# Batch 0's token-major scores computed by TensorE, first loads in longer rows, opening reordered: an attention and feed-forward kernel on one core

## The chip, the core and the metric

The kernel runs on one core of one Trainium2 chip. The metric is the device time of one execution in microseconds, the median of several runs. The core's engines are named as in the profile: PE (TensorE; PEld are its weight loads), DVE (VectorE), ACT (ScalarE), POOL (GpSimd) and SP (SyncE, here only an issuer of DMAs).

## What is computed

```python
B, H, S, Ns, D = (8, 8, 512, 32, 64)            # x: B,H,S,D   state: B,H,Ns,D
def _attn_ref(x, state):
    scores = scale * x @ state.T                 # tokens look at 32 state rows
    a = softmax(scores); xread = a @ state
    scores2 = scale * state @ x.T                # state rows look at 512 tokens
    a2 = softmax(scores2); sread = a2 @ x
    return concatenate([xread, sread], axis=2)   # B,H,544,D

def _moe_ref(x, w_in, w_out):                    # x: 4352 rows of 512
    h = x @ w_in                                 # 512 x 2048, float64 in memory
    g = h - tanh(h)
    return g @ w_out                             # 2048 x 512, float64 in memory
```

The attention output, with its heads joined, is the input of the feed-forward layer. Inputs x and state are float32, the two weight matrices are float64 and are turned to float32 on the chip.

## The kernel before

The feed-forward layer works through nine chunks of rows: eight batches of 512 tokens (chunks 0 to 7) and, last, the 256 rows that the state rows give. Each chunk has 16 hidden tiles (a 128-row piece of the 2048 hidden features): `hidden` makes h of one tile on PE, ACT makes tanh, DVE subtracts, and `output` multiplies with a row block of w_out. Products with state are folded into w_in: m = state times w_in, so that the attention weights multiply m directly. The whole program is built once; a scheduler sets the order on each engine, except where `tc.keep_in_program_order` or `tc.issue_after` pins it.

The change is in the opening, before the first hidden tile of chunk 0. Its order is written out by hand: `SEQ` is a string of two-letter steps, a letter for the operation and a number for its piece, and `step` issues each. What is shown as `tps`, `sps`, `mps` and so on in the rows are PSUM tiles of these steps:

- D: a matmul on zeros (`warm`), which only keeps PE busy.
- S0, S1: scores of batch 0 with state rows in partitions (`sps`), for heads 0 to 3 and 4 to 7: two matmuls of 128x64 weights (a block-diagonal `bdr` of state) and 512 columns each. c0, c1: ACT copies them to SBUF (`s`).
- T0, T1: the same scores with tokens in partitions (`tps`). In the kernel before these are four 128x128 transposes of the copy `s` (line 735).
- M, B, E, Z, z, q, N: softmax over the 32 state rows: DVE maximum (line 738), DVE subtraction (`e`, line 742), ACT exponential, DVE sum, add, reciprocal, DVE scaling (line 753).
- A, y: four PE transposes back (`aps`, line 758) and ACT's copy to `at`.
- a, b, r, p: the four instructions that turn one float64 weight block to float32: two integer operations on DVE (lines 136 and 137), one on ACT (line 138, tiles named w00r, wo0r and so on), one custom sum on DVE (line 139). Numbers 0 to 3 are the first 512 columns of w_in (blocks w00 to w03), 4 and 5 the first two row blocks of w_out (wo0, wo1). A `p` of 0 to 3 also writes the converted block to DRAM (`wf`), for use much later, and every `p` issues the next weight load.
- m, k, R: m of the first 512 hidden features on PE (`mps`, lines 792 and 783) and ACT's copies of it to SBUF.
- h0 to h3, H0 to H3: hidden tiles 0 to 3 of chunk 0 (`hps`, line 808), first and second half of the heads. X is their tanh, x their subtraction (`g`, line 815). After them PE goes on with `output` of chunk 0 (`ops`, line 604 and following).

All loads of the opening are on SP's DMA queue, but for one of 256 KB on ACT's. A weight block lands in one of six raw buffers (`parts`, four, and `twins`, two), so a load waits on SP until the block that was in its buffer is converted, and everything behind it on SP waits with it. The converted blocks are written to two rotating tiles (tag `wf`, two buffers of two blocks each): whoever writes such a tile again waits until its DRAM writes have been read out.

Of the kernel before, what the change touches and what calls it, by code (L numbers as in the profile page):

```python
# [9 lines left out]
F32 = mybir.dt.float32  # L10
# [27 lines left out]
@with_exitstack  # L38
def attention_ffn(ctx: ExitStack, tc: tile.TileContext, xT, xn, x0, bh, sp, sm, win, wout, xout, tout, sout):

# [47 lines left out]
    def bank(p, name):  # L88
        return p.tile([P, 512], F32, tag=p.name, name=name)
# [7 lines left out]
    def big(name, shape, dtype):  # L97
        return pool.tile(shape, dtype, tag="big", name=name, bufs=BIG)
# [7 lines left out]
    class Weight:  # L106
# [4 lines left out]

        def load(self):
            if self.src.dtype == F32:
                self.raw = next(raws)(f"{self.name}d", [P, 512], F32)
                dst = self.raw
            else:
                self.raw = next(raws)(f"{self.name}d", [P, 512, 2], U32)
                dst = self.raw.rearrange("p f w -> p (f w)")
            src = self.src.bitcast(dst.dtype)
            if len(src.shape) == 3:  # L120
                dst = dst.rearrange("p (r f) -> p r f", r=4)
            loadlog.append(nc.sync.dma_start(dst, src).ins)

# [518 lines left out]
    def advance(units, n=1):  # L642
# [7 lines left out]
    w0 = [  # L650
        [Weight(win[r * P : r * P + P, 512 * q : 512 * q + 512], f"w{q}{r}") for r in range(DM // P)]
        for q in range(NQ)
    ]

    w0[0] = [
        Weight(win[:, j * P : j * P + P].rearrange("(r p) f -> p r f", p=P), f"w0{j}") for j in range(4)
    ]
    wos = [Weight(wout[f * P : f * P + P], f"wo{f}") for f in range(NFF)]
    wfs = {}

    def convert_win(q, p):
        if p % 2 == 0:
            wfs[q, p // 2] = pool.tile([P, 2, 512], F32, tag="wf", name=f"w0{q}{p // 2}", bufs=WB)
        made = w0[q][p].convert(wfs[q, p // 2][:, p % 2])
        if p % 2:
            nc.sync.dma_start(wf[q][:, p - 1 : p + 1], wfs[q, p // 2])
        return made
# [18 lines left out]
    def o(x):  # L686
        tc.keep_in_program_order(x)
        if x.ins.engine == mybir.EngineType.DVE:
            firstDVE[0] = x.ins

    aTs[0] = pool.tile([P, 2, 2, 512], F32R, tag="aT0", name="aT0", bufs=1)
    sps = pool.tile([P, 4, P], F32, tag="sm", name="sps", bufs=1)
    xb = big("x00", [P, 768], F32)
    xrs = [pool.tile([P, 2, 512], F32, tag="x", name=f"xT0{hf}", bufs=XB) for hf in range(2)]
    nc.sync.dma_start(xb, x0)
    nc.scalar.dma_start(xrs[0][:, 1], xT[0, 0][:, 1])
    load(1)
    nc.sync.dma_start(xrs[1], xT[0, 1])
    nc.sync.dma_start(sps, sp[0])
    load(4)  # L700
    bdr = xb[:, :256].rearrange("p (i m) -> p i m", i=4)
    moving = {(0, 0): xb[:, 256:]} | {(j, c): xrs[j][:, c] for j, c in ((0, 1), (1, 0), (1, 1))}

# [13 lines left out]
    def step(op):  # L717
# [3 lines left out]
        elif k == "S":  # L721
            sps_ps[j] = bank(ps_o, f"sps0{j}")
            for c in range(2):
# [6 lines left out]
        elif k == "T":  # L730

            tps[j] = bank(ps_o, f"tps0{j}")
            for t in range(4):
                cols = slice(P * t, P * t + P)
                o(nc.tensor.transpose(tps[j][:, cols], ss[j][:, cols], ident))
        elif k == "M":
# [25 lines left out]
        elif k in "abrp":  # L762
            if j not in csteps:
                if j > 3:
                    if j == 4:
                        plain[0] = big("wp0", [P, 2, DM], F32)
                    csteps[j] = wos[j - 4].steps(plain[0][:, j - 4])
                else:
                    if j % 2 == 0:
                        wb[j // 2] = pool.tile([P, 2, 512], F32, tag="wf", name=f"w00{j}", bufs=WB)  # L770
                    csteps[j] = w0[0][j].steps(wb[j // 2][:, j % 2])
# [3 lines left out]
            if k == "p" and j < 4:  # L775
                w = wb[j // 2][:, j % 2].rearrange("p (r f) -> p r f", r=4)
                nc.sync.dma_start(wf[0][:, :, j * P : j * P + P], w)
        elif k == "m":
# [41 lines left out]
    MP = [{"a": ps_a, "o": ps_o}[x] for x in 'oaoa']  # L820
    SEQ = 'D D D D D b0 S0 D a0 c0 T0 S1 D M0 r0 B0 p0 m0 E0 c1 r1 Z0 T1 R0 b1 a1 z0 p1 q0 a2 k0 b2 r2 N0 m1 p2 A0 r3 M1 k1 R1 y0 r4 b3 B1 a3 m2 E1 p3 Z1 r5 h1 h0 m3 k2 z1 q1 h2 N1 A1 a5 k3 y1 h3 R2 b4 H0 R3 b5 H1 X0 H2 X1 a4 H3 p5 p4 x0 x1'
    for op in SEQ.split():
# [521 lines left out]
```

## Time and profile before

| | |
|---|---|
| median of 3 runs | 629.43 us (629.32 to 630.81) |
| the profiled execution: its own time | 629.0 us |
| its span (first to last instruction) | 627.2 us |
| PE busy | 621.5 us, 99% of the span, 3610 matmul records |
| DVE busy | 488.8 us, 78% |
| ACT busy | 370.4 us, 59% |
| POOL busy | 38.7 us, 6% |

A float32 matmul leaves two records in the trace (two passes), a transpose and a matmul on float32r operands one. PE's records have a modelled end; the distance between starts tells how fast it works. A row of the timeline can merge several records of one kind, with their number behind the x; its duration is from the first start to the last end. Idle time before a row stands in brackets with what ended it.

### The profile page before, as it was taken

Reading aid. Unit: us, or ns where it says so; the run is one execution under the profiler, and the core shown is the slowest. Engines: PE = TensorE matmul, PEld = TensorE weight load, DVE = VectorE, ACT = ScalarE, POOL = GpSimd, SP = SyncE. Lnnn points to the kernel's source line nnn. Section 1 sums busy time; section 2 is a strip of 40 time slices with the busy share of each in tenths; the row PEclk is TensorE's granted clock in tenths of the full one; section 3 lists DMA queues with packets and bytes.
Section 4 is the critical chain, followed back from the end, with each engine's and each line's share of the span. In section 5 each row is a group of like instructions: output and inputs, shape, how many; then the busy total and the mean of one; then the engine's idle time right before and its main releaser. Section 6 shows DMA issues by size and latency. Waiting matters only on the chain.

```text
span 627.2 us, 9849 instructions
## 1 busy us (share of the span) xinstructions
PE 621.5 (99%) x3610; PEld 490.9 (78%) x3610; DVE 488.8 (78%) x781; ACT 370.4 (59%) x613; POOL 38.7 (6%) x66
## 2 busy tenths in 40 slices
PE   8999999999999999999999999999999999999997
PEld 5456677788888788778886678788888888888997
DVE  5999998799697696998357679988955878764582
ACT  5876777678666475755346785447555543562642
POOL 0000002132311000000000000000000000010000
PEclk9999999999999999999999999999999999999999
DMA  9993875869988857999716996765555675699990
GB/s 318 354 390 135 302 245 145 256 194 341 291 278 287 280 177 262 319 315 397 253 34 217 338 345 212 228 209 168 176 168 183 201 187 164 201 260 341 410 337 26
DMA packets 68672, 155.90 MB, mean 249 GB/s; under 512 B 6032, under 2 KB 27920, under 8 KB 68624
## 3 DMA queue, kind: packets, MB, share of 16 engines
q1 hardware_dynamic: 62400, 134.04, 63.7%
q0 software_dynamic: 6080, 20.98, 11.5%
q8 instruction: 28, 0.46, 0.3%
q10 hardware_dynamic: 144, 0.26, 0.1%
q14 instruction: 20, 0.16, 0.1%
HBM read 110.69 MB, written 44.56 MB: 248 GB/s over the span
## 4 chain that ended last, share of the span: by engine, by line
PE 96%; DVE 2%; ACT 1%; issue 0%; ACTq 0%
PE X L1067 14%; PE hps L553 10%; PE hps L554 10%; PE hps L555 10%; PE ops L606 8%; PE ops L608 8%; PE ops L607 8%; PE Y0m L1067 5%; PE Y1m L1067 5%; PE mps L263 2%; PE mps L179 2%; PE X L1173 2%; PE ops L604 2%; PE Y8m L1173 1%; PE rps L501 1%; PE hps L808 1%
## 5 line engine op out<-in xcount | busy, mean ns | idle before, releaser
L606 PE MATMUL ops<-wo,g 128*128 128x512 f32 x244 | 95.5, 396 | 0.0
L607 PE MATMUL ops<-wo,g 128*128 128x512 f32 x244 | 95.2, 390 | 0.0
L553 PE MATMUL hps<-aT,m 128*128 128x512 f32 x240 | 94.7, 397 | 0.0
L554 PE MATMUL hps<-aT,m 128*128 128x512 f32 x240 | 93.8, 391 | 0.1
L555 PE MATMUL hps<-aT,m 128*128 128x512 f32 x240 | 93.8, 391 | 0.0
L608 PE MATMUL ops<-wo,g 128*128 128x512 f32 x244 | 88.3, 393 | 0.0
L568 ACT ACTIVATE t<-hps 128x512 f32<-128x512 f32 x64 | 38.4, 601 | 57.9 <-PE hps L555 57.2
L568 DVE TENSOR_TENSOR G<-hps,t 128x512 f32<-128x512 f32 x64 | 43.8, 687 | 36.8 <-ACT t L568 36.7
L606 PEld LDWEIGHTS ops<-wo,g 128*128 128x128 f32 x244 | 45.7, 188 | 15.6 <-issue 1.9
L553 PEld LDWEIGHTS hps<-aT,m 128*128 128x128 f32 x240 | 45.0, 188 | 14.5 <-issue 2.5
L580 DVE TENSOR_TENSOR t<-hps,t 128x512 f32<-128x512 f32 x61 | 41.7, 683 | 18.4 <-ACT t L580 18.0
L104 ACT CAST g<-t 128x512 fp32r<-128x512 f32 x61 | 37.8, 619 | 28.5 <-DVE t L580 27.9
L608 PEld LDWEIGHTS ops<-wo,g 128*128 128x128 f32 x244 | 45.6, 188 | 10.8 <-DVE wo L104 0.8
L555 PEld LDWEIGHTS hps<-aT,m 128*128 128x128 f32 x240 | 45.0, 188 | 11.0 <-issue 1.7
L607 PEld LDWEIGHTS ops<-wo,g 128*128 128x128 f32 x244 | 45.8, 188 | 9.9 <-DVE wo L104 0.3
L554 PEld LDWEIGHTS hps<-aT,m 128*128 128x128 f32 x240 | 45.1, 188 | 9.7 <-DVE aT L104 0.5
L580 ACT ACTIVATE t<-hps 128x512 f32<-128x512 f32 x61 | 36.4, 597 | 26.3 <-PE hps L555 25.9
L1067 PE MATMUL X<-g0m,W0m 128*128 128x512 f32 x192 | 47.9, 390 | 0.0
L104 DVE TENSOR_TENSOR g<-t,g 128x512 fp32r<-128x512 f32 x61 | 41.6, 684 | 7.1 <-ACT g L104 6.9
L1067 PE MATMUL X<-g1m,W1m 128*128 128x512 f32 x192 | 45.8, 389 | 0.0
L104 ACT CAST g1m<-G 128x1024 fp32r<-128x1024 f32 x28 | 29.2, 1056 | 27.6 <-PE Y1m L1067 10.9
L1067 PEld LDWEIGHTS X<-g0m,W0m 128*128 128x128 f32 x192 | 36.0, 188 | 8.3 <-issue 0.8
(279 smaller groups left out, 1155.4 us busy)
## 6 DMA issues: line engine op xcount, KB each, us to landing
w<-wf POOLq DMA_DIRECT2D x32, 256.0 KB, 6.5
mm<-st POOLq DMA_DIRECT2D x16, 512.0 KB, 6.3
xn<-in_xn SPq DMA_DIRECT2D x16, 512.0 KB, 5.8
mr<-mm SPq DMA_DIRECT2D x16, 512.0 KB, 5.1
wsd<-ws SPq DMA_DIRECT2D x16, 512.0 KB, 7.7
wod<-wo SPq DMA_DIRECT2D x32, 256.0 KB, 6.6
W0m<-wsd SPq DMA_DIRECT2D x16, 512.0 KB, 3.7
W1m<-wsd SPq DMA_DIRECT2D x16, 512.0 KB, 3.9
```

What stands on the lines that cost most here:

```text
L104: return nc.scalar.copy(hi, src), (sub or nc.vector).tensor_sub(lo, src, hi)
L179: made = nc.tensor.matmul(pss[b][rows], sp2[r, p + c, 64 * b + at : 64 * b + at + 32], w[r, c], start=True, stop=True,)
L553: nc.tensor.matmul(ps, mhi[k][:, cols], ahi[:, k], start=(k == 0), stop=False)
L554: nc.tensor.matmul(ps, mhi[k][:, cols], alo[:, k], start=False, stop=False)
L555: made = nc.tensor.matmul(ps, mlo[k][:, cols], ahi[:, k], start=False, stop=(k == nk - 1))
L568: main(nc.scalar.activation(t, ps, AF.Tanh), nc.vector.tensor_sub(g, ps, t))
L580: tanhs.append((nc.scalar.activation(t, ps, AF.Tanh).ins, nc.vector.tensor_sub(t, ps, t).ins))
L606: nc.tensor.matmul(o, g[:, 0, tok], w[:, 0], start=(f in self.begins), stop=False)
L607: nc.tensor.matmul(o, g[:, 0, tok], w[:, 1], start=False, stop=False)
L608: return nc.tensor.matmul(o, g[:, 1, tok], w[:, 0], start=False, stop=stop).ins
L1067: made = nc.tensor.matmul(out[t], w[:, e, x, cols], y[:, e], start=first and j == 0 and e == 0 and c == 0, stop=last and j == 3 and e == 1 ...
L1173: made = nc.tensor.matmul(out, o[:, x, s], w[:, y], start=first and jp == 0 and s == 0 and c == 0, stop=last and jp == 1 and s == 3 and c ...
```

## The change

Batch 0's x arrives in one load of 640 KB with the block-diagonal state ahead of it (128 rows of 5 KB), in place of 384 KB on SP's queue and 256 KB on ACT's. Weight block w00 goes to ACT's queue instead. The first 512 columns of w_in come as an input of their own, laid out so that each of w00 to w03 is 128 rows of 4 KB in place of 512 rows of 1 KB. T0 and T1 are eight matmuls each of x (the stationary operand, 128 tokens) with the block-diagonal state (64 columns), straight from the loaded x; the copies c0 and c1 remain for the state rows' own softmax, which comes later. The DRAM writes of w00 to w03 go from SP's queue to POOL's (`pooled`). Block w10 (the next columns of w_in) gets its four steps in the opening as number 6. The string SEQ has a new order with two steps D fewer.

```diff
-        def load(self):
+        def load(self, queue=nc.sync):
...
-            loadlog.append(nc.sync.dma_start(dst, src).ins)
+            loadlog.append(queue.dma_start(dst, src).ins)
...
-    w0[0] = [
-        Weight(win[:, j * P : j * P + P].rearrange("(r p) f -> p r f", p=P), f"w0{j}") for j in range(4)
-    ]
+    w0[:0] = [[
+        Weight(w0b[j], f"w0{j}") for j in range(4)
+    ]]
...
-    xb = big("x00", [P, 768], F32)
-    xrs = [pool.tile([P, 2, 512], F32, tag="x", name=f"xT0{hf}", bufs=XB) for hf in range(2)]
+    xb = pool.tile([P, 1280], F32, tag="aT1", name="x00", bufs=1)
+    xr = pool.tile([P, 2, 512], F32, tag="x", name="xT01", bufs=XB)
     nc.sync.dma_start(xb, x0)
-    nc.scalar.dma_start(xrs[0][:, 1], xT[0, 0][:, 1])
-    load(1)
-    nc.sync.dma_start(xrs[1], xT[0, 1])
+    next(loads).load(nc.scalar)
+    nc.sync.dma_start(xr, xT[0, 1])
...
-            sps_ps[j] = bank(ps_o, f"sps0{j}")
+            sps_ps[j] = bank(ps_h, f"sps0{j}")
...
             for t in range(4):
-                cols = slice(P * t, P * t + P)
-                o(nc.tensor.transpose(tps[j][:, cols], ss[j][:, cols], ident))
+                for c in range(2):
+                    cols = slice(P * t + 64 * c, P * t + 64 * c + 64)
+                    o(nc.tensor.matmul(
+                        tps[j][:, cols], moving[j, c][:, P * t : P * t + P], bdr[:, 2 * j + c], start=True, stop=True
+                    ))
...
-                if j > 3:
-                    if j == 4:
+                if j == 6:
+                    wfs[1, 0] = pool.tile([P, 2, 512], F32, tag="wf", name="w010", bufs=WB)
+                    csteps[j] = w0[1][0].steps(wfs[1, 0][:, 0])
+                elif j > 3:
+                    if 0 not in plain:
...
-                nc.sync.dma_start(wf[0][:, :, j * P : j * P + P], w)
+                pooled(wf[0][:, :, j * P : j * P + P], w)
...
-    SEQ = 'D D D D D b0 S0 D a0 c0 T0 S1 D M0 r0 B0 p0 m0 E0 c1 r1 Z0 T1 R0 b1 a1 z0 p1 q0 a2 k0 b2 r2 N0 m1 p2 A0 r3 M1 k1 R1 y0 r4 b3 B1 a3 m2 E1 p3 Z1 r5 h1 h0 m3 k2 z1 q1 h2 N1 A1 a5 k3 y1 h3 R2 b4 H0 R3 b5 H1 X0 H2 X1 a4 H3 p5 p4 x0 x1'
+    SEQ = 'D D D D D r0 T0 b0 a0 M0 S0 B0 p0 T1 m0 E0 r1 Z0 a1 r2 b1 z0 p1 b2 q0 R0 a2 r3 S1 m1 c0 k0 N0 p2 A0 y0 M1 a3 B1 b3 m2 k1 c1 h1 h0 p3 R1 E1 k2 Z1 z1 r6 q1 r4 m3 N1 h2 k3 A1 h3 y1 H0 b5 a5 r5 R3 X0 H1 R2 H2 a6 a4 b4 p4 b6 X1 x0 H3 p5 x1'
...
-            turn = convert_win(1, p)
+            turn = convert_win(1, p, csteps.get(6) if p == 0 else None)
...
-    x0 = c(np.concatenate([bd[0].reshape(P, 256), xT[0, 0, :, 0]], axis=1))
+    x0 = c(np.concatenate([bd[0].reshape(P, 256), xT[0, 0].reshape(P, 2 * S)], axis=1))
...
+    w0b = c(win[:, :512].reshape(4, P, 4, P).transpose(2, 1, 0, 3).reshape(4, P, 512))
+    win = c(win[:, 512:])
```

On PE, from the first matmul to the first hidden tile, these stand in a row before (tps 135 and 168 are T0 and T1, sps S0 and S1, mps 153, 190 and 223 m0 to m2, aps 203 is A0, hps 1 is h1):

```order
L720 MATMUL warm<-const-float32-0.0 128x256 x5
L724 MATMUL sps_128<-x_101 64x512
L724 MATMUL sps_128<-xT_102,x_101 64x512
L720 MATMUL warm<-const-float32-0.0 128x256
L735 MATMUL tps_135<-ident,s_133 128x128 x4
L724 MATMUL sps_140<-xT_103,x_101 64x512 x2
L720 MATMUL warm<-const-float32-0.0 128x256
L792 MATMUL mps_153<-w_125,sps 64x128 x8
L735 MATMUL tps_168<-ident,s_133 128x128 x4
L792 MATMUL mps_190<-w_125,sps 64x128 x8
L758 MATMUL aps_203<-ident,e_147 128x128 x4
L783 MATMUL mps_223<-w_183,sps 128x128 x4
```

And these now:

```order
L717 MATMUL warm<-const-float32-0.0 128x256 x5
L733 MATMUL tps_126<-x_101 128x64 x8
L721 MATMUL sps_139<-x_101 64x512 x2
L733 MATMUL tps_148<-x_101,xT_102 128x64 x8
L795 MATMUL mps_157<-w_123,sps 64x128 x8
L721 MATMUL sps_188<-xT_102,x_101 64x512 x2
L795 MATMUL mps_191<-w_123,sps 64x128 x8
L758 MATMUL aps_208<-ident,e_142 128x128 x4
L786 MATMUL mps_221<-w_172,sps 128x128 x4
```

T0 and T1 moved ahead of the S of their half and depend on loads alone; from A0 (`aps`) on, PE's order is the same to the program's end.

On ACT, around y1 (the second copy to `at`, line 761), which H0 waits for, these stand before:

```order
L138 ACTIVATE w10r<-w10d 128x512
L803 COPY mr_119<-mps_241 64x2x128 x2
L761 COPY at_261<-aps_253 128x512
L803 COPY mr_173<-mps_223 64x2x128 x2
L803 COPY mr_173<-mps_241 64x2x128 x2
L811 ACTIVATE t_0_273<-hps_0_239 128x512
L811 ACTIVATE t_1_276<-hps_1_237 128x512
L138 ACTIVATE w11r<-w11d 128x512
```

And these now:

```order
L136 ACTIVATE w10r<-w10d 128x512
L136 ACTIVATE wo0r<-wo0d 128x512
L806 COPY mr_117<-mps_250 64x2x128 x2
L136 ACTIVATE w11r<-w11d 128x512
L761 COPY at_267<-aps_260 128x512
L136 ACTIVATE wo1r<-wo1d 128x512
L806 COPY mr_183<-mps_250 64x2x128 x2
L814 ACTIVATE t_0_276<-hps_0_230 128x512
```

The conversion of block w11 moved from behind the first two tanh to the place just ahead of y1.

On DVE, from the second half's scaling (N1, line 753) to the first subtraction `g_0`, which the first `output` matmul waits for, these stand before:

```order
L753 TENSOR_TENSOR e_220<-e_220,z_233 128x512
L136 TENSOR_SCALAR wp_216<-wo1d 128x512
L137 TENSOR_SCALAR wo0r<-wo0d 128x512
L137 TENSOR_SCALAR wo1r<-wo1d 128x512
L136 TENSOR_SCALAR wp_216<-wo0d 128x512
L139 ISA wp_216<-wp_216,wo1r 128x1024
L139 ISA wp_216<-wp_216,wo0r 128x1024
L815 TENSOR_TENSOR g_0_286<-hps_0_239,t_0_273 128x512
```

And these now:

```order
L753 TENSOR_TENSOR e_218<-e_218,z_240 128x512
L135 TENSOR_SCALAR wo1r<-wo1d 128x512
L134 TENSOR_SCALAR wp_247<-wo1d 128x512
L134 TENSOR_SCALAR w_243<-w10d 128x512
L134 TENSOR_SCALAR wp_247<-wo0d 128x512
L135 TENSOR_SCALAR wo0r<-wo0d 128x512
L137 ISA wp_247<-wp_247,wo0r 128x1024
L135 TENSOR_SCALAR w10r<-w10d 128x512
L818 TENSOR_TENSOR g_0_291<-hps_0_230,t_0_276 128x512
```

Two instructions of block w10 moved ahead of `g_0`. The first of them (`w_243<-w10d`, step a6) writes the tile that held w00 and w01, so it waits for the two DRAM writes of these blocks, which are now on POOL's queue.

## Rows read from the trace of the kernel before

**Rows 1.** The page's chain that ended last, shares of the span by engine

```profile
PE 96%; DVE 2%; ACT 1%; issue 0%; ACTq 0%
```

**Rows 2.** Timeline of PE, first 22 us: start, duration (us), engine, line, operation, tiles

```profile
0.78 4.53 PE L720 MATMUL warm<-const-float32-0.0 128*128 128x256 f32 x10 [0.78 <-PEq L1329]
...
7.23 0.63 PE L735 MATMUL tps<-ident,s 128*128 128x128 f32 x4
8.40 1.08 PE L724 MATMUL sps<-xT,x 128*64 128x512 f32 x4 [0.54 <-DMA xT<-in_xT]
...
10.04 1.09 PE L792 MATMUL mps<-w,sps 128*64 128x128 f32 x16
...
13.73 0.63 PE L758 MATMUL aps<-ident,e 128*128 128x128 f32 x4 [0.38 <-DVE e L753]
14.33 1.13 PE L783 MATMUL mps<-w,sps 128*128 128x128 f32 x8
...
18.96 0.60 PE L758 MATMUL aps<-ident,e 128*128 128x128 f32 x4
```

**Rows 3.** The same view from 19 to 66 us

```profile
23.77 7.03 PE L604 MATMUL ops<-wp,g 128*128 128x512 f32 x16
...
54.92 0.61 PE L553 MATMUL hps<-aT,m 128*128 128x512 f32 x2
55.62 0.50 PE L554 MATMUL hps<-aT,m 128*128 128x512 f32 x1
```

**Rows 4.** Timeline of DVE, first 40 us

```profile
6.99 0.47 DVE L137 TENSOR_SCALAR w00r<-w00d 128x512 uint16<-128x512 uint16 x1 [6.99 <-DMA w00d<-in_win]
...
7.90 0.69 DVE L738 TENSOR_REDUCE m<-tps 128x16 f32<-128x512 f32 x1
...
12.91 0.68 DVE L753 TENSOR_TENSOR e<-e,z 128x512 f32<-128x512 f32 x1
...
18.01 0.69 DVE L753 TENSOR_TENSOR e<-e,z 128x512 f32<-128x512 f32 x1
18.62 0.42 DVE L136 TENSOR_SCALAR wp<-wo1d 128x512 uint32<-128x512 uint32 x1
18.95 0.46 DVE L137 TENSOR_SCALAR wo0r<-wo0d 128x512 uint16<-128x512 uint16 x1
...
22.38 1.29 DVE L815 TENSOR_TENSOR g<-hps,t 128x512 f32<-128x512 f32 x2 [1.13 <-ACT t L811]
```

**Rows 5.** Timeline of ACT, first 40 us

```profile
19.59 0.59 ACT L761 COPY at<-aps 128x512 f32<-128x512 f32 x1 [0.47 <-PE aps L758]
```

**Rows 6.** Timeline of SP's DMA queue, first 40 us

```profile
0.74 0.38 SPq L695 DMA_DIRECT2D x<-in_x  x1
...
11.45 0.34 SPq L122 DMA_DIRECT2D w11d<-in_win  x1
```

**Rows 7.** DMA issues, first 40 us: size, median us from issue to landing

```profile
wf<-w SPq DMA_DIRECT2D x4, 256.0 KB, 7.7
...
w11d<-in_win SPq DMA_DIRECT2D x1, 512.0 KB, 7.9
...
x<-in_x SPq DMA_DIRECT2D x1, 384.0 KB, 4.4
```

**Rows 8.** Table of stretches: PE, PEld, DVE, ACT, POOL busy, PEclk, DMA share, GB/s

```profile
0.00:4.00 4.00, 3.22 (x8) 2.62 (x9) 0.00 (x0) 1.28 (x1) 0.70 (x6) 1.00 0.51 148
4.00:5.50 1.50, 1.50 (x6) 0.84 (x6) 0.00 (x0) 0.00 (x0) 0.00 (x0) 1.00 1.03 328
5.50:7.00 1.50, 1.50 (x6) 0.38 (x4) 0.01 (x1) 0.50 (x2) 0.00 (x0) 1.00 1.03 397
```

**Rows 9.** DMA queues from 3 to 3.5 us (q1 SP's, q10 ACT's): packets, MB

```profile
q1 hardware_dynamic: 34, 0.10, 62.5%
q10 hardware_dynamic: 32, 0.07, 34.5%
```

**Rows 10.** The page's DMA issues from POOL's queue

```profile
w<-wf POOLq DMA_DIRECT2D x32, 256.0 KB, 6.5
```

More of the change, by code (lines that the diff above doesn't have):

```diff
@@ L38, in attention_ffn @@
 @with_exitstack
-def attention_ffn(ctx: ExitStack, tc: tile.TileContext, xT, xn, x0, bh, sp, sm, win, wout, xout, tout, sout):
+def attention_ffn(ctx: ExitStack, tc: tile.TileContext, xT, xn, x0, bh, sp, sm, w0b, win, wout, xout, tout, sout):
     nc = tc.nc
@@ L119, in load @@
             src = self.src.bitcast(dst.dtype)
-            if len(src.shape) == 3:
-                dst = dst.rearrange("p (r f) -> p r f", r=4)
-            loadlog.append(nc.sync.dma_start(dst, src).ins)
+            loadlog.append(queue.dma_start(dst, src).ins)
         def steps(self, dst):
@@ L650, in attention_ffn, with convert_win @@
     w0 = [
-        [Weight(win[r * P : r * P + P, 512 * q : 512 * q + 512], f"w{q}{r}") for r in range(DM // P)]
-        for q in range(NQ)
-    ]
-    w0[0] = [
-        Weight(win[:, j * P : j * P + P].rearrange("(r p) f -> p r f", p=P), f"w0{j}") for j in range(4)
-    ]
+        [Weight(win[r * P : r * P + P, 512 * q - 512 : 512 * q], f"w{q}{r}") for r in range(DM // P)]
+        for q in range(1, NQ)
+    ]
+    w0[:0] = [[
+        Weight(w0b[j], f"w0{j}") for j in range(4)
+    ]]
     wos = [Weight(wout[f * P : f * P + P], f"wo{f}") for f in range(NFF)]
     wfs = {}
-    def convert_win(q, p):
-        if p % 2 == 0:
+    def convert_win(q, p, begun=None):
+        if p % 2 == 0 and begun is None:
             wfs[q, p // 2] = pool.tile([P, 2, 512], F32, tag="wf", name=f"w0{q}{p // 2}", bufs=WB)
-        made = w0[q][p].convert(wfs[q, p // 2][:, p % 2])
+        made = begun[3]().ins if begun else w0[q][p].convert(wfs[q, p // 2][:, p % 2])
         if p % 2:
@@ L701, in attention_ffn @@
     bdr = xb[:, :256].rearrange("p (i m) -> p i m", i=4)
-    moving = {(0, 0): xb[:, 256:]} | {(j, c): xrs[j][:, c] for j, c in ((0, 1), (1, 0), (1, 1))}
+    moving = {(0, c): xb[:, 256 + 512 * c : 768 + 512 * c] for c in range(2)} | {(1, c): xr[:, c] for c in range(2)}
     warm = bank(ps_a, "warm")
@@ L1327 @@
     win, wout = (c(w).view(np.int64) if w.dtype == np.float64 else w for w in (moe_w_in, moe_w_out))
+    w0b = c(win[:, :512].reshape(4, P, 4, P).transpose(2, 1, 0, 3).reshape(4, P, 512))
+    win = c(win[:, 512:])
     nc = bacc.Bacc("TRN2", target_bir_lowering=False, num_devices=1, dynamic_dma_scratch_size=1024)
-    arrays = {"in_xT": xT, "in_xn": xn, "in_x0": x0, "in_bh": bh, "in_sp": sp, "in_sm": sm, "in_win": win, "in_wout": wout}
+    arrays = {"in_xT": xT, "in_xn": xn, "in_x0": x0, "in_bh": bh, "in_sp": sp, "in_sm": sm, "in_w0": w0b, "in_win": win, "in_wout": wout}
     args = [
```

## The prediction

> **What bounds the kernel now.** I read the chain that ended last first: 96% of it is PE [rows 1]. So the end moves with the moment from which PE never waits again, and with whatever makes it wait later. The timeline of PE shows that moment. Before A0 at 13.73 PE has gaps, filled with matmuls on zeros, and A0 itself waited 0.38 us for DVE [rows 2]. From A0 on I find only one more: at 55 us two records start 0.23 us apart and the next is due at about 55.37, but starts at 55.62 [rows 3]; it waits for DVE's split of batch 1's attention. The sum is therefore: how far A0 and the first `output` matmul (23.77 [rows 3]) move, less the 0.25 us that a later PE would no longer wait at 55 us. DVE is the other engine to watch. It has nothing to do until w00 lands at 6.99, takes its first maximum (M0) at 7.90, scales at 12.91 (N0) and 18.01 (N1), and from 7.9 to 21.2 it has next to no gap; then it is idle for 1.13 us [rows 4]. The DMA engines are full from 4 us on (share 1.03 [rows 8]).
>
> **When x lands.** Before, the 384 KB with the state and half of x are issued at 0.74 and land 4.4 us later, at 5.1 [rows 6, 7]; the other half came beside it on ACT's queue. Between 3 and 3.5 us SP's queue moved 34 packets and ACT's 32 [rows 9]: the two queues take turns, packet by packet. Now 655 kB on SP's queue stand beside 524 kB of w00 on ACT's, both in 128 rows. The first 4 us move 592 kB (148 GB/s), after that long rows move 397 kB/us and 1 KB rows 328 [rows 8]. If x went first, it would be through at 4.0 + 63/397 = 4.2; if all of w00 went with it, at 4.0 + 587/397 = 5.5. Before, 393 kB of x and about 200 kB of the other queue were through at 4.0 and the landing was seen 1.14 us later. So x lands between 5.3 and 6.6. I take 6.4, near the upper end, because the packets alternate and ACT's queue only starts some packets later. The first S and T could start at 5.2 before; that is 1.2 us lost. w00 itself lands at about 6.7 in place of 6.98.
>
> **T0 and T1 by matmul.** Removed from the path: S0, the copy c0, four transposes; T0 ended at 7.23 + 0.63 = 7.86 [rows 2]. Added: eight matmuls, 16 records, each with new 128-column weights and only 64 columns to stream. No row has that shape. The nearest is m2, full weights with 128 columns: 8 records in 1.13 us, 0.12 apart; transposes are 0.11 to 0.12 apart too [rows 2]. Records with 64-column weights (m0) are 0.054 apart [rows 2], which gives 16 x 0.054 = 0.9, and with the tail 1.1, as the lower bound; if weights and columns did not overlap, 0.11 + 0.053 each gives 2.6. I take 16 x 0.11 = 1.76 and 0.2 of tail, since the full weights are what m2 and the transposes share. T0 then runs from 6.44 to 8.4, and M0 starts at 8.45 in place of 7.90: **0.55 us later**. A smaller load, a shorter chain, and still later, because the data come later.
>
> **From M0 to A0.** DVE's list between M0 and N0 has the same eleven instructions, so N0 starts at 8.45 + (12.91 - 7.90) = 13.46, and A0, 0.82 us behind N0 before, at 14.2 to 14.3. Would PE be there in time? Its list from 6.44 is T0 1.76, S0 1.0 (four records in 1.08), T1 1.76, m0 0.9, S1 1.0, m1 0.9 [rows 2]: 7.3 us, free at 13.8. So DVE still decides, by half a microsecond. If T cost 2.6, PE would: 6.44 + 9.0 = 15.4, and A0 would be 1.7 us late. The two steps D that go away were cover for nothing that waits.
>
> **From A0 to the first output.** PE's order is the same, so 0.5 to 0.55 us carry through: h, m3, A1, H0, `output` at about 24.3. Two moved pieces stand beside this. First, ACT now converts w11 just ahead of y1. w11 landed at 11.45 + 7.9 = 19.35 [rows 6, 7]; y1 would start at 19.59 + 0.55 = 20.15 [rows 5], and the conversion needs 0.64 before it, so it is hidden if w11 lands by 19.45. Four blocks in long rows save up to 4 x 524 x (1/328 - 1/397) = 1.1 us of the queue; one more DRAM write (262 kB) shares the engines with it now, 0.7 us. I leave it at 19.35, so it costs nothing, but it also caps any gain: y1 not before 20.0. Second, step a6 ahead of `g_0`, which is the first rival below. The writes that leave SP's queue unblock the loads behind them, but these wait for their buffers anyway. The steps of w10 fill DVE's idle 1.13 us; nothing that PE waits for in the next 30 us is nearer than about a microsecond, except the attention at 55 us. DVE reaches that at the old time, PE 0.55 later, so its 0.25 us of waiting go. PE then runs to the end without a gap to absorb the rest.
>
> **Sum.** 0.55 - 0.25 = 0.3 us. The profiled execution took 629.0, its span 627.2 and 1.8 around it, which the change doesn't touch; it would take 629.3. That execution is 0.4 below the median of the runs, 629.43, to which I add the same: 629.7.
>
> **Rival 1, slower: a6 waits for POOL's queue.** a6 must find both DRAM writes of w00 and w01 done, and behind it on DVE stand 0.33 + 0.33 + 0.35 for wo0 (two-operand integer steps 0.33 apart [rows 4]), 0.60 for its sum, 0.35 for w10 and 0.68 for `g_0`: 2.64 us, until which PE cannot start `output` at 24.3. So a6 may start up to 21.6. p0 is the third DVE step from M0 and ends at 8.45 + 0.72 + 0.61 + 0.69 = 10.5; p1 ends 0.7 ahead of N0, at 12.8. POOL's writes of this size land 6.5 us after issue, the same writes from SP's queue 7.7 [rows 7, 10]: 19.3 to 20.5, in time. But the first of them here have 512 short rows each and share full DMA engines, and if the second only starts when the first is through, they land at 10.5 + 13 = 23.5 to 10.5 + 15.4 = 25.9; `output` starts at 26.2 to 28.6, and with the 0.25 the kernel gets 2.2 to 4.6 us slower, about 632.8. It turns slower than before when a6 starts after 21.3.
> The Trainium skill (SBUF — State Buffer, section on the two sides of SBUF) has a rule against this edit: a DMA issued from GpSimd can't get its descriptors written while VectorE runs an instruction that takes both ports. No row here shows it, since POOL issues nothing in the opening before. By the page's example, 0.62 us becoming 3.1, my estimate is 2.5 us on the second write, 23.0, and 1.4 us above my forecast, 631.1; it would be a smaller form of this rival.
>
> **Rival 2, the gain arrives.** x is served first (5.3) and T0 costs 1.1. Then M0 waits for w00 and its two integer steps, 7.45, 0.45 ahead of before, and A0 comes at 13.3. But H0 still needs y1 behind w11: 20.6, against 20.2 before. Only with w11 at 18.9 or earlier does the gain survive. Together 0 to -0.4: 629.0 to 629.4. For it speaks that w00 lands a little sooner; against it the alternating packets.
>
> **Rival 3, PE is slow in the opening.** Weights and columns don't overlap (A0 1.7 late, 1.45 net, 630.9), or the clock falls. The warm-up records, 256 columns, start some 0.44 us apart (10 in 4.53) [rows 2], as the 512-column ones of `output` do (16 in 7.03) [rows 3]: that is the lower of the two levels, 1.2 GHz. PE now has nothing between 5.3 and x's landing, where before S0 followed at 5.2. At the lower level T0 to m1 take 14.6 in place of 7.3 and A0 comes 7 us late: 636. The granted clock reads 1.00 throughout [rows 8], so I give that little.
> That the change does not do what it says is part of the forecast: the DMA engines are full, so longer rows hardly bring x sooner.
>
> **How the numbers follow.** Chances: forecast 0.65 (629.0 to 631.0 with x between 6.0 and 6.6 and T between 1.3 and 2.2), rival 2 0.17, rival 1 0.10, rival 3 0.06 (0.02 of it the clock), a gain that I don't see 0.02. A measurement of this kernel tells about 0.3% from no change, 1.9 us: below 627.5 or above 631.3. Faster 0.02; slower takes most of rival 1, the clock and a little of the rest, 0.11; same 0.87. The range holds the forecast, rival 2 and the nearer ends of rivals 1 and 3: 628.7 to 631.6. Likeliest 629.7.
>
> **What would show it.** Right: x lands after 6 us, T0's records 0.11 apart, M0 at 8.3 to 8.6, A0 about half a microsecond later than 13.73, `output` at about 24.3, no wait of PE at 55 us. Wrong: M0 before 7.9; T0's 16 records in under 1.2 us; DVE waiting ahead of w10's first step; ACT waiting for w11 with y1 behind it; PE's records 0.2 us and more apart in T0.

## The result and the profile after

| | before | after |
|---|---|---|
| median of 7 runs each, same chip | 630.51 us (628.70 to 631.00) | 634.21 us (632.37 to 635.96) |
| ratio | | 1.0063, 95% interval 1.0050 to 1.0076 |
| the profiled execution: its own time, its span | 629.0, 627.2 us | 632.54, 630.8 us |
| PE busy | 621.5 us | 623.2 us |

The change makes the kernel 0.6% slower. The prediction, 629.7 us with a range of 628.7 to 631.6, was wrong.

The executions of the kernel after do not lie around one value. Two stand at 632.4 and 632.5 with a mean granted clock of 1.0, four at 634.2 with a clock of 0.992, and one at 635.96 whose clock reads 1.0. The kernel before has none like these: its executions lie between 628.5 and 632.2 us in every comparison below. The profile shows one of the two at 632.5. So there are two questions: what the 3.5 us of that execution are, and what brings the others to 634 and 636.

For the first, the chain of work that ended last in the profile after, shares by engine, against [rows 1]:

```profile
PE 87%; DVE 5%; DMA 5%; ACT 2%; issue 1%; DVEq 0%; ACTq 0%
```

PE no longer sets the end alone; DVE and DMA have come in. The same chain between 15 and 45 us names the DMA (start us, us, what):

```profile
16.63 5.59 DMA wf<-w
...
22.41 0.43 DVE w L134
...
24.91 0.57 DVE g L818
...
28.03 5.28 DMA wf<-w
...
33.50 0.43 DVE w L134
```

Two DRAM writes of POOL's queue lie on the path, and each is followed by a DVE step that overwrites the tile which was written out. The timeline of POOL gives the issues of all four writes (start, duration, engine, line; in brackets the idle time before):

```profile
10.27 1.05 POOL L305 DMA_DIRECT2D wf<-w  x1 [8.96 <-DVE w L137]
16.63 0.73 POOL L305 DMA_DIRECT2D wf<-w  x1 [5.31 <-DVE w03r L135]
22.52 0.91 POOL L305 DMA_DIRECT2D wf<-w  x1 [5.16 <-issue]
28.03 0.89 POOL L305 DMA_DIRECT2D wf<-w  x1 [4.59 <-DVE w11r L135]
```

Block w01 was converted at 12.4 (second row of DVE below), and its write was issued at 16.63. The step of w03 that the bracket names there has nothing to do with w01. The four go out one at a time, 5.5 to 6.4 us apart. They land 6.1, 5.6, 5.2 and 5.3 us after their issues, so each is issued about 0.3 us after the one ahead of it has landed (16.4, 22.2, 27.7). The timeline of DVE, against [rows 4]:

```profile
7.93 0.69 DVE L738 TENSOR_REDUCE m<-tps 128x16 f32<-128x512 f32 x1 [1.12 <-PE tps L733]
...
11.75 0.69 DVE L137 CUSTOM_DVE_ANT_0 w<-w,w01r 128x1024 uint16<-128x1024 uint16 x1
...
19.25 0.41 DVE L134 TENSOR_SCALAR wp<-wo1d 128x512 uint32<-128x512 uint32 x1
22.41 0.43 DVE L134 TENSOR_SCALAR w<-w10d 128x512 uint32<-128x512 uint32 x1 [2.75 <-DMA wf<-w]
...
24.80 0.68 DVE L818 TENSOR_TENSOR g<-hps,t 128x512 f32<-128x512 f32 x1
```

DVE stood for 2.75 us in front of step a6, with `g_0` 2.39 us behind it. The timeline of PE, against [rows 2, 3], with what that does:

```profile
5.89 2.00 PE L733 MATMUL tps<-x 128*128 128x64 f32 x16 [0.71 <-DMA x<-in_x]
...
13.97 0.63 PE L758 MATMUL aps<-ident,e 128*128 128x128 f32 x4 [0.38 <-DVE e L753]
...
25.62 4.96 PE L602 MATMUL ops<-wp,g 128*128 128x512 f32 x11 [1.23 <-DVE g L818]
...
42.32 1.98 PE L549 MATMUL hps<-at,mr 128*128 128x512 f32 x4 [1.28 <-ACT mr L226]
```

`output` starts at 25.62 in place of 23.77, 1.85 us later. At 42.32 PE has waited a second time, for ACT. The timeline of ACT there:

```profile
41.16 0.62 ACT L104 CAST wo<-wor 128x512 fp32r<-128x512 f32 x1 [1.15 <-DVE wor L137]
41.69 0.58 ACT L226 COPY mr<-mps 128x512 f32<-128x512 f32 x1
```

The copy of `mr`, which PE wanted at 40.9, stands behind a cast of a row block of w_out, and that waited for DVE, which was late by then. 1.85 and 1.28 make 3.1 of the 3.6 us of span; the rest is in small waits that I didn't follow one by one.

### The profile page after: what moved, and what is told of

It reads as the page before. It is cut to its first block, busy times and chain, and to the rows that moved or that the text cites. A ratio compares the mean times of both kernels' runs of the same rounds, so it can differ in the third digit from the quotient of the medians.

```text
span 630.8 us, 9885 instructions
## 1 busy us (share of the span) xinstructions
PE 623.2 (99%) x3630; PEld 492.8 (78%) x3630; DVE 489.7 (78%) x781; ACT 369.8 (59%) x613; POOL 42.2 (7%) x70
## 4 chain that ended last, share of the span: by engine, by line
PE 87%; DVE 5%; DMA 5%; ACT 2%; issue 1%; DVEq 0%; ACTq 0%
PE X L1070 12%; PE hps L551 9%; PE hps L553 9%; PE hps L552 9%; PE ops L604 9%; PE ops L606 9%; PE ops L605 9%; PE Y1m L1070 5%; PE Y0m L1070 5%; PE mps L261 2%; DMA md<-sl 2%; PE X L1176 2%; DMA wf<-w 2%; PE Y8m L1176 1%; PE rps L499 1%
```

## The experiments

Lines and names are those of the kernel after, if nothing else is said. Times are medians, in brackets lowest to highest; ratios are to the kernel before on the same chip, with 95% intervals. The runs were spread over four chips (e1 to e4, e5 to e8, e9 to e11, e12), on which the kernel before has medians of 629.29, 628.99, 629.23 and 629.03 us, against 630.51 in the table above; across these groups the ratios are the safer comparison.

| run | edit | us | ratio |
|---|---|---|---|
| e1 | after, writes on SP | 635.20 (630.13 to 636.18) | 1.0076 (1.0048 to 1.0104) |
| e2 | after, scratch 2048 | 629.97 (629.53 to 636.93) | 1.0031 (0.9996 to 1.0066) |
| e3 | after without step 6 | 632.92 (630.98 to 634.36) | 1.0048 (1.0026 to 1.0070) |
| e4 | before, writes on POOL | 634.74 (634.34 to 635.57) | 1.0082 (1.0066 to 1.0099) |
| e5 | after, six D | 632.64 (632.54 to 634.44) | 1.0064 (1.0051 to 1.0077) |
| e6 | e2 with four D | 634.88 (634.25 to 635.62) | 1.0092 (1.0079 to 1.0106) |
| e7 | e2, x and w00 on one queue | 630.76 (630.15 to 632.00) | 1.0029 (1.0018 to 1.0041) |
| e8 | before, T by matmul | 629.72 (629.08 to 630.10) | 1.0006 (0.9997 to 1.0015) |
| e9 | e2 with six D | 630.19 (629.83 to 631.24) | 1.0017 (1.0008 to 1.0026) |
| e10 | e8 with the long loads | 629.92 (629.32 to 630.94) | 1.0008 (0.9999 to 1.0016) |
| e11 | e7 with w10, w11 later | 629.83 (629.33 to 630.71) | 1.0009 (1.0000 to 1.0018) |
| e12 | e10 with c0, c1 later | 629.85 (629.12 to 631.32) | 1.0015 (1.0006 to 1.0024) |

### e1: the writes back on SP's queue

```diff
-                pooled(wf[0][:, :, j * P : j * P + P], w)
+                nc.sync.dma_start(wf[0][:, :, j * P : j * P + P], w)
```

> The changed kernel with one thing undone: the four writes of w00 to w03 go to DRAM from SP's queue, as before the change, and not from POOL's. PE, DVE and ACT keep every instruction in the place that the change gave it. Theory A (POOL's writes go one at a time and hold the buffer that VectorE's first step of w10 wants): the wait of 2.75 us ahead of that step at 19.7 to 22.4 us falls under 0.5 us, TensorE's stall ahead of `ops` (1.39 us) goes, and so does the one at 40.65 us (1.44 us), if it is only the first one handed on; the time falls by about 2.8 us, to 631.0 +-0.6. Theory B (the new order on VectorE and ScalarE costs by itself, whoever writes): both stalls stay, 633.5 to 634.5. Theory C: the first stall goes and the second stays, since a cast of `wo` now stands ahead of the copy of `mr` on ScalarE: 632.5 to 633.

One execution of six took 630.13 us, a little below the 630.4 to 631.6 of theory A; the five others took 634.4 to 636.2, so that the median says nothing against B. The profiled execution, one of 636.18, showed a cause that none of the theories had. Its timeline of PE:

```profile
5.84 3.67 PE L733 MATMUL tps<-x 128*128 128x64 f32 x16 [0.45 <-DMA x<-in_x]
9.44 1.98 PE L721 MATMUL sps<-x 128*64 128x512 f32 x4
```

The same 16 records that took 2.00 us in the profile after take 3.67 here, and the four of S0 1.98 in place of 1.08: TensorE is at its lower level (1.2 GHz). It stays there until A0 at 20.19, in place of 13.97. On DVE step a6 follows its predecessor without a wait, at 25.56. This became theory C: behind the warm-up matmuls PE stands idle until x lands (0.45 us here, 0.71 in the profile after), where before S0 followed at once, and in some executions the clock does not rise, or falls again. By theory C the 634 and 636 of the kernel after are such executions; none of these was profiled.

### e2: room for two writes

```diff
-    nc = bacc.Bacc("TRN2", target_bir_lowering=False, num_devices=1, dynamic_dma_scratch_size=1024)
+    nc = bacc.Bacc("TRN2", target_bir_lowering=False, num_devices=1, dynamic_dma_scratch_size=2048)
```

> The changed kernel with one number changed: the scratch that POOL's transfers take for their descriptors is 2048 bytes a partition in place of 1024. No instruction moves. Theory A1 (the second write is not issued because the first one's 512 descriptors fill that scratch until it has drained): the second write is issued at 12.4 to 13.0 us in place of 16.63 and lands by 19; the wait ahead of w10's first step falls from 2.75 us to under 0.5; 631 to 632. Theory A2 (VectorE's work keeps POOL's descriptors from being written, the trap of the shared port): the issues stay 5 us apart and the time at 634.

POOL's timeline and the DVE step:

```profile
10.17 1.07 POOL L305 DMA_DIRECT2D wf<-w  x1 [8.87 <-DVE w L137]
12.67 0.74 POOL L305 DMA_DIRECT2D wf<-w  x1 [1.43 <-DVE w L137]
14.64 0.90 POOL L305 DMA_DIRECT2D wf<-w  x1 [1.23 <-DVE w L137]
17.50 0.72 POOL L305 DMA_DIRECT2D wf<-w  x1 [1.96 <-DVE w L137]
```

```profile
19.50 0.42 DVE L134 TENSOR_SCALAR w<-w10d 128x512 uint32<-128x512 uint32 x1
```

No instruction moved, and each write is now issued as soon as its block is converted. a6 starts at 19.50 without a wait, `output` at 24.17, and PE's timeline names no wait at 40 us any more: the second stall was the first one handed on. Four of six executions took 629.5 to 630.2, against 632.4 for the best of the kernel after. So A1 holds, with a time about 1 us below the 631 to 632 that I expected: the size of that scratch makes POOL's writes go one at a time. That one write's descriptors fill it is my reading; no row counts them.

The Trainium skill (SBUF — State Buffer, section on the two sides of SBUF) would put the late issues down to VectorE's two-port instructions, which keep GpSimd from writing descriptors. These runs speak against it as the cause here: DVE's work is the same in both kernels, and the second issue moved from 16.63 to 12.67.

The two other executions took 634.2 (clock 0.992) and 636.93 (clock 1.0), where theory C would put them.

### e3: step 6 left to the scheduler

```diff
-    SEQ = '... k1 Z1 z1 r6 q1 ... R2 H2 a6 a4 b4 p4 b6 X1 x0 H3 p5 x1'
+    SEQ = '... k1 Z1 z1 q1 ... R2 H2 a4 b4 p4 X1 x0 H3 p5 x1'
```

> The changed kernel with the first steps of w10 (on VectorE and ScalarE) taken out of the order written by hand: they are left to the scheduler, as before the change, which puts them behind `g_1`. The writes stay on POOL. Theory A: nothing ahead of `g_0` waits for a write, so `ops` starts at 24.0 to 24.4 us and its stall goes; w10's steps still wait till about 22.4, so the stall at 40 us may stay in part; 631 to 633. Theory B (the order as a whole costs): 634.

The first stall goes: `output` starts at 24.05. The other write to the same tile keeps its price, and PE pays it later. DVE, then PE:

```profile
32.50 0.43 DVE L134 TENSOR_SCALAR w<-w12d 128x512 uint32<-128x512 uint32 x1 [1.03 <-DMA wf<-w]
```

```profile
57.20 0.73 PE L551 MATMUL hps<-aT,m 128*128 128x512 f32 x2 [0.94 <-ACT aT L104]
```

The best two executions took 631.0 and 631.1, between e2 and the kernel after, as theory A expected. Against the best of the kernel after, a6's place makes some 1.4 of the 3.5 us; it is not the root.

### e4: POOL's writes in the kernel before

```diff
-                nc.sync.dma_start(wf[0][:, :, j * P : j * P + P], w)
+                pooled(wf[0][:, :, j * P : j * P + P], w)
```

> The kernel before with one thing of the change: the four writes of w00 to w03 are issued by POOL. PE, DVE and ACT keep their order. Theory A: the writes go out one at a time, about 5.5 us apart from 10 us on, so the two of w00 and w01 are through at about 22 us and w10's first step, which stands behind `g_1` here, starts at 24 to 25 us at the latest as it did; the first `ops` still starts at 23.8; only w12's steps (buffer of w02 and w03, free at about 33.5) are late, which costs 0 to 1.5 us: 630.5 to 632. Theory B (writes harmless): 630.5 +-0.4.

This one edit costs 5.4 us between the medians, far more than I expected, and all of six executions show it. The fourth write is issued only at 27.45, and DVE stands 4.53 us before the first step of w12 (35.27). The row names a load of wo6, which this step doesn't read; w12 itself had landed at 22.3, and the fourth write landed 7.6 us after its issue, at 35.05. PE and its clock, from the timeline and the table of stretches (PE busy, granted clock, DMA share, GB/s):

```profile
38.73 1.96 PE L179 MATMUL mps<-w,sps 64*32 64x512 f32 x16 [2.28 <-DVE w L139]
```

```profile
35.00:40.00 5.00, 2.72 (x20) 0.85 0.83 256
40.00:45.00 5.00, 4.92 (x26) 0.81 0.92 288
```

PE waits 2.28 us, and behind the wait the granted clock falls: the 16 records take 1.96 us in place of 1.09. The 1.09 is that of e2 and of undisturbed rows in e4. The 2.28 us and the 1.7 us that the two stretches lose by their clock make 4.0 of the 6.6 us by which this execution's span is longer than the kernel before's (633.8 against 627.2); I didn't follow the rest. Three of the six executions show a clock of 1.0 and took 634.6 to 635.5 all the same. So the writes alone cost the kernel before no less than the whole change does.

### e5 and e6: one warm-up matmul more, one fewer

e5 is the kernel after with this edit:

```diff
-    SEQ = 'D D D D D r0 T0 ...'
+    SEQ = 'D D D D D D r0 T0 ...'
```

e6 is e2 with this one:

```diff
-    SEQ = 'D D D D D r0 T0 ...'
+    SEQ = 'D D D D r0 T0 ...'
```

> The changed kernel with one warm-up matmul more (six `D` in place of five) ahead of the first T; POOL's writes stay as they are. In the profile of e1 TensorE ran the opening at half speed (16 records of T in 3.67 us against 2.00) until 20 us, after it had stood idle for 0.45 us between the warm-up and the first T. Theory C (the idle time behind the warm-up lets TensorE go on at its lower level for the opening in some executions, and these are the executions of 634 to 636 us): with the gap filled no execution is above 633; all stand at 632.2 to 632.8, and T0 starts within 0.2 us of 5.9. Theory A alone (POOL's writes make all of the difference): the spread stays, 632.4 to 636, median 634.

> The kernel of e2 (scratch for descriptors doubled) with one warm-up matmul fewer (four `D`). TensorE's idle time ahead of the first T grows from about 0.8 us to about 1.5. Theory C: nearly every execution has the opening at half speed: median 634 to 637, none or one under 631; in the profile the 16 records of T take 3.6 us and TensorE is slow until about 20 us. If the gap has nothing to do with it: four of six at 629.5 to 630.3, as e2.

With six, three of five executions took 632.5 to 632.6, one 633.4 and one 634.4 with a clock of 0.997; none shows 0.992 or 636. Two lie above the 633 that theory C had as the limit, so the spread is not all gone. With four, all of four took 634.3 to 635.6, where e2, with five, had four of six at 629.5 to 630.2. So the number of warm-up matmuls sets how often the time is lost, in the direction of theory C. The profile of e6, PE and the stretches (PE busy, granted clock, DMA share, GB/s):

```profile
5.92 2.00 PE L733 MATMUL tps<-x 128*128 128x64 f32 x16 [1.39 <-DMA x<-in_x]
7.85 1.87 PE L721 MATMUL sps<-x 128*64 128x512 f32 x4
9.65 3.68 PE L733 MATMUL tps<-x,xT 128*128 128x64 f32 x16
```

```profile
6.00:8.00 2.00, 2.00 (x18) 1.00 1.04 416
8.00:10.00 2.00, 2.00 (x6) 0.50 1.05 424
...
16.00:18.00 2.00, 2.00 (x16) 0.50 1.01 408
18.00:20.00 2.00, 1.99 (x19) 0.94 1.04 412
```

Here the clock had risen (T0 takes 2.00 us), and fell to 0.50 between 8 and 18 us, after 1.39 us of idle time. Ten us at 0.50 cost 5 of some 632, or 0.8%. This execution's mean clock is 0.991, and the four of the kernel after at 634.2 show 0.992: they fit a loss of this kind. The forecast of the details was off: I expected T0 slow, as in e1. There are two ways to lose the clock, and they cost the opening 4.5 us (A0 at 18.44 here, at 13.90 in e2) to 6.2 us (e1). In e5's profile the sixth matmul did not fill the gap: PE was idle for 0.98 us and kept its clock. So the length of the gap alone does not tell; with more warm-up ahead of it the loss was rarer.

### e9: both causes taken away

```diff
-    ... dynamic_dma_scratch_size=1024)
+    ... dynamic_dma_scratch_size=2048)
-    SEQ = 'D D D D D r0 T0 ...'
+    SEQ = 'D D D D D D r0 T0 ...'
```

> The changed kernel with both causes taken away and nothing else: the scratch for POOL's descriptors doubled (as e2) and six warm-up matmuls in place of five (as e5). If A and C together are the whole of the loss, every execution lies at 629.3 to 630.4, median 629.7, 0.1% from before at most; if either stays (executions of 632.5 or of 634 and more), something else is at work too.

All eleven executions took 629.8 to 631.2, with a median 0.5 us above the 629.7 that I expected and four of them above 630.4. The executions of 632.5 and those of 634 and more are gone. Two edits, of one number and one matmul, bring the loss from 0.63% down to 0.17%, or 1.0 us. Its profile says where: T0 starts at 6.03, behind the sixth warm-up matmul, A0 at 14.38 and `output` at 24.66, 0.89 later than [rows 3].

### e7 and e11: x and w00 on one queue

e7 is e2 with this edit:

```diff
-    next(loads).load(nc.scalar)
+    load(1)
```

e11 is e7 with the first steps of w10 behind `p4`, and those of w11 as a new number 7:

```diff
-    SEQ = '... R2 H2 a6 a4 b4 p4 b6 X1 x0 H3 p5 x1'
+    SEQ = '... R2 H2 a4 b4 p4 a6 b6 X1 r7 x0 H3 p5 x1 a7 b7'
```

> The kernel of e2 with w00 loaded by SP's queue right behind x, and not by ScalarE's queue beside it. PE, DVE and POOL keep their order. x need no longer share the transfers with w00: it should land at 5.0 to 5.4 us in place of 5.8, w00 at 6.0 to 6.4; T0 then follows the warm-up without a gap (ends at 7.2), and `M0` starts at 7.3 to 7.9. Theory C: no execution at half speed, all within 628.9 to 629.9, the median 0 to 0.4 us under e2's fast ones. If x lands no earlier, the gap and the spread stay as in e2.

> The kernel of e7 (new order, scratch doubled, x and w00 on one queue) with two steps moved: VectorE's first steps of w10 stand behind the last step of wo0, and ScalarE's step of w11 stands behind the tanh of hps1, not ahead of the copy `y1`. In e7's profile `y1` waited for w11 (landed at 20.99), and `hps` stalled for 1.5 us behind it. Theory: that stall goes, the first aps is at 13.3 and `ops` starts at 23.3 to 23.7: 628.6 to 629.2. If TensorE then waits for another load, 629.5 to 630.5.

On one queue x landed 3.5 us after its issue, at 4.2, in place of 5.84; T0 follows the warm-up at 5.2 and `M0` starts at 7.29. No execution shows a lost clock in the opening (630.15 to 632.0; lowest mean clock 0.997). That fits theory C, too. But the 628.9 to 629.9 that I expected did not come, since the gain went to a new wait, ACT and PE in e7 (the profiled execution is the slowest, 632.0):

```profile
20.99 0.78 ACT L136 ACTIVATE w11r<-w11d 128x512 uint16<-128x512 uint32 x1 [1.37 <-DMA w11d<-in_win]
21.64 0.56 ACT L761 COPY at<-aps 128x512 f32<-128x512 f32 x1
```

```profile
22.25 4.97 PE L811 MATMUL hps<-at,mr 128*128 128x512 f32 x7 [1.45 <-ACT at L761]
```

Behind this wait, and one of 0.60 us that ended at 19.68, the clock fell (stretches of e7: PE busy, granted clock, DMA share, GB/s):

```profile
22.00:24.00 2.00, 1.75 (x3) 0.65 0.17 37
24.00:26.00 2.00, 2.00 (x3) 0.50 0.91 287
```

With w11's conversion behind the tanh (e11) this wait is gone, but `output` starts at 24.21 where I expected 23.3 to 23.7: PE now waits 0.40 us at 19.81 for ACT's copy of `mr`. The time, 629.83, is no better than before.

### e8, e10 and e12: the parts that cost little

e8 is the kernel before with T0 and T1 by matmul, as in the change, and T0 ahead of S0; e10 adds the longer rows of x and w00 to w03, on SP's queue:

```diff
-    SEQ = 'D D D D D b0 S0 D a0 c0 T0 S1 D M0 ...'
+    SEQ = 'D D D D D b0 T0 a0 S0 D c0 S1 D M0 ...'
```

e12 is e10 with the copies c0 and c1 later; r0 and M0 come ahead of S0, y0 ahead of R1, and one D goes:

```diff
-    SEQ = 'D D D D D b0 T0 a0 S0 D c0 S1 D M0 r0 B0 p0 m0 E0 c1 r1 ... p2 A0 r3 M1 k1 R1 y0 r4 ...'
+    SEQ = 'D D D D D r0 T0 b0 a0 M0 S0 B0 p0 S1 D m0 E0 r1 ... p2 A0 c0 r3 M1 k1 y0 R1 c1 r4 ...'
```

> The kernel before with one thing of the change: T0 and T1 are made by TensorE straight from x and the tokens (16 records each) in place of copy and transposes, T0 ahead of S0. Loads, writes and the order of VectorE and ScalarE stay as before. T0 follows the warm-up at about 5.2 us without a gap and ends at about 7.2; `M0` is then held only by VectorE's two steps of w00 (to 7.76 us), so it starts at 7.75 to 7.9 where it started at 7.90: 628.7 to 629.6, within 0.1% of before in every theory; if T took something away from the later work, over 630.

> The kernel before with two things of the change, and neither of the two that cost: T0 and T1 straight from TensorE (order as e8) and the first loads in longer rows, x and w00 one behind the other on SP's queue (as e7). The writes of w00 to w03 stay on SP's queue, the new order of VectorE and ScalarE is left out. VectorE's first steps of w00 should start at 5.9 in place of 6.99 and M0 at 7.3 in place of 7.90, so the first aps at 13.1 to 13.4 in place of 13.73. If the gain of 0.4 to 0.6 us arrives at TensorE: 628.4 to 628.8, 0.05 to 0.1% faster than before. If a later wait takes it (w10 or w11, which come at the pace of the transfers): 628.9 to 629.3.

> The kernel of e10 with the copies of the first scores (`c0`, `c1`) moved on ScalarE from ahead of w00's step to behind w02's and behind `y0`. In e10's profile VectorE's last step of w00 waited 0.90 us for ScalarE's step of w00, which stood behind the copy of the first scores; that ate the gain of the earlier loads. Theory: that wait goes, the first aps is at 13.0 to 13.4 (before 13.73), `ops` starts at 23.1 to 23.6 (before 23.77), and the time is 0.2 to 0.6 us under before: 628.7 to 629.0. If a later row takes it (w10 or w11 landing, the cast ahead of hps4), 629.2 to 629.6, no difference that can be measured.

e8 shows no difference clear of the noise, and no gain. M0 came earlier (7.34), but DVE lost it again at the last step of w00, which waited for ACT behind the copy c0. Its profile also shows a price of the matmuls. PE:

```profile
11.40 2.00 PE L736 MATMUL tps<-x,xT 128*128 128x64 f32 x16
13.33 1.09 PE L795 MATMUL mps<-w,sps 128*64 128x128 f32 x16
14.35 0.66 PE L761 MATMUL aps<-ident,e 128*128 128x128 f32 x4
```

T1 takes 2.00 us, where the transposes of T1 took 0.66 in the kernel before, and in this order it stands between m0 and m1. PE has no gap ahead of A0 any more: A0 comes at 14.35 in place of 13.73, `output` at 24.07, 0.30 later. In the kernel after T1 stands ahead of m0, and A0 waits for DVE as it did before. e10 lost M0's gain at the same place as e8, DVE and ACT:

```profile
9.95 0.69 DVE L137 CUSTOM_DVE_ANT_0 w<-w,w00r 128x1024 uint16<-128x1024 uint16 x1 [0.90 <-ACT w00r L136]
```

```profile
8.65 0.59 ACT L726 COPY s<-sps 128x512 f32<-128x512 f32 x1 [6.63 <-PE sps L721]
9.13 0.78 ACT L136 ACTIVATE w00r<-w00d 128x512 uint16<-128x512 uint32 x1
```

e12 takes that wait away, and M0 starts at 6.43, 1.5 us ahead of [rows 4]. DVE, then PE:

```profile
6.43 0.69 DVE L738 TENSOR_REDUCE m<-tps 128x16 f32<-128x512 f32 x1
...
9.82 0.47 DVE L135 TENSOR_SCALAR w01r<-w01d 128x512 uint16<-128x512 uint16 x1 [0.59 <-DMA w01d<-in_w]
...
12.12 0.68 DVE L753 TENSOR_TENSOR e<-e,z 128x512 f32<-128x512 f32 x1
...
16.77 0.69 DVE L747 TENSOR_REDUCE z<-e 128x16 f32<-128x512 f32 x1 [0.67 <-ACT e L744]
```

```profile
10.60 2.00 PE L733 MATMUL tps<-x,xT 128*128 128x64 f32 x16
12.53 1.09 PE L795 MATMUL mps<-w,sps 128*64 128x128 f32 x16
13.55 0.66 PE L758 MATMUL aps<-ident,e 128*128 128x128 f32 x4
...
23.83 6.60 PE L602 MATMUL ops<-wp,g 128*128 128x512 f32 x15
```

Now w01 is late: it lands at 9.8, with the DMA engines full (share 0.97 to 1.04 from 4 us on). At N0 0.8 of the 1.5 us are left (12.12 against 12.91). A0 then waits for PE and not for DVE: T1 and m1 fill PE up to 13.55, so 0.18 us are left there. By N1 (17.99 against 18.01) the rest is gone: DVE waited 0.67 us for ACT's exponential, which now stands behind c1 and wo0's conversion. `output` starts at 23.83 against 23.77. I expected 628.7 to 629.0 and got 629.85. The spans show no such loss (medians 627.4 and 627.3 us); the device time has 2.4 us outside the span in place of 1.8, and no profile shows why. No version that I ran beats the kernel before.

## Why the prediction was wrong, point by point

- **Rival 1, the failed step.** The mechanism, the place and the work behind it stood in the prediction, as a rival: a6 waits for POOL's writes, and from a6 to `g_0` it took 2.39 us (I had 2.64). The step that failed is "19.3 to 20.5, in time". It took POOL's two writes as overlapping, from rows of writes elsewhere [rows 10] that say how long one takes and nothing of the distance between two. The second was issued at 16.63, when the first was through, and a6 started at 22.41, later than the 21.3 that I had as the limit. I had written that very case down, with 2.2 to 4.6 us, and gave the rival 0.10 where it had no row against it. That its 632.8 meets the 632.5 of the profiled execution is partly luck: the two writes took 6.1 and 5.6 us and not 6.5 to 7.7, so `output` came at 25.62, ahead of the rival's 26.2 to 28.6, and the second wait, which the rival did not have, made up for it.
- **The same step, its second half.** I followed the writes of w00 and w01 only. Those of w02 and w03 go out third and fourth, and w12's steps wait for them (0.67 us in the profile after, 1.03 in e3, 4.53 in e4). And "nothing that PE waits for in the next 30 us is nearer than about a microsecond" gave no cover to a DVE that is 3 us late (w12's first step at 33.50 in place of 30.42): at 42.32 PE has waited 1.28 us behind a cast on ACT. e2, where both go with the writes, shows that they are one cause.
- **Rival 3, the clock.** It had the right place, "PE now has nothing between 5.3 and x's landing", and 636 as its price, which is that of the whole opening at the lower level (e1); four of the five executions concerned stand at 634.2. I gave it 0.02 because the granted clock of the kernel before read 1.00 throughout [rows 8]; but that kernel has no such gap, so its rows could not speak to it, and the column reads 1.00 over my own warm-up records, which I had found at the lower level. By their times and clocks it happened in five of seven executions. It does not seem to add to rival 1: the kernel after and e2 alike have executions at 634.2 with a clock of 0.992. My reading is that where the opening is 5 us late anyway, the writes are through in time; no profile of the kernel after in that state shows it.
- **x's landing, mis-sized.** I took 6.4 within bounds of 5.3 to 6.6; x landed at 5.84. In e7, with w00 behind it on the same queue, it landed at 4.2.
- **T0 by matmul, right.** 16 records 0.11 to 0.12 apart, 2.00 us, where I had 1.96.
- **M0 and A0, mis-sized.** M0 at 7.93 in place of 8.45, for x's sake; A0 at 13.97, +0.24 where I had +0.5.
- **w11 ahead of y1, nearly right.** y1 started at 20.09, for which I had 20.15. I called it free; since A1 came earlier than forecast, PE waited about a quarter of a microsecond for it.
- **The wait at 55 us, right.** It is nearly gone: the record behind the two starts 0.53 us after them (58.43 and 58.96), where it was 0.70 [rows 3].
- **Without the two rivals** the sum came out, partly by luck. The four executions of e2 at 629.5 to 630.2 are the change without either: their median is 629.7, 0.4 above before on that chip, with `output` at 24.17; I had 0.3 and 24.3. But two errors offset each other: x landed 0.56 us earlier than I took, and the step y1 behind w11, free in my sum, cost about a quarter of a microsecond. e9, with a sixth warm-up matmul, is 1.0 us above before; A0 and `output` come 0.5 us later there than in e2.

## What to carry to other kernels

A transfer moved to another queue comes under that queue's own limits: ask how many can be in flight at once, and give every instruction that overwrites the source the time of all the writes ahead of it, one behind the other, unless a row shows two overlapping. Where a stage starts only when a load lands, ask what PE does up to that moment: in these runs a gap behind the warm-up lost the clock in some executions, and one more matmul (e5, e9) or an earlier landing (e7) made that rarer or took it away. The single executions, not only the median, show whether it did. An earlier start of one chain is worth only what the other engines leave of it: in e12 the next block's landing, PE's longer list and the order on ACT took all of 1.5 us.

## What the runs showed of the hardware

- With 1024 bytes of descriptor scratch, POOL's four writes were issued 5.5 to 6.4 us apart, each about 0.3 us after the one ahead had landed; with 2048 (e2), 0.3 to 0.4 us after the end of each conversion, with the one ahead still under way.
- TensorE's level in the opening differs from execution to execution of one program: with an idle gap of 0.45 to 1.39 us behind 3.75 to 4.61 us of warm-up matmuls, the clock either stays (the profiles of the kernel after, e2, e3 and e5), falls to 0.50 for 10 us (e6), or the records run at the lower level from the start until 20 us (e1). The Trainium skill (TensorE: Matmul & The Clock Gate, Part 1) says that the moment of the rise varies from run to run; these traces agree: the same ten warm-up matmul records take 4.19 us in e2 and 4.61 in e3. The Trainium skill (TensorE: Matmul & The Clock Gate, Part 1) also puts the loss by the ramp under 1% of a typical kernel's span. Here the executions at 634.2 lie 1.7 us (0.3%) above the best two of the kernel after, and one of e2, which was not profiled, lies 7 us (over 1%) above the others (636.93 against 629.7).
- In e1's profile the granted clock reads 1.00 for the whole opening while T0's 16 records take 3.67 us in place of 2.00. There the distance between records told the level, and the column did not.
- In the middle of dense work the clock fell behind a wait of PE of 2.28 us in e4 (0.85 and 0.81 over the two stretches of 5 us around and behind it) and behind waits of 0.60 and 1.45 us in e7 (0.65 and 0.50 over the next 4 us). It stayed at 1.00 behind waits of 1.23 and 1.28 us in the profile after and of 1.79 us in e5 (at 42.57), so these waits give no limit.
